# Three slot arrays and bank turns in the order list of a fused attention and MLP kernel

## The chip, the cores and the metric

The kernel runs on one core of a Trainium2 chip. The metric is the device time of one execution in microseconds (us), as the median over several runs. The engines named below are PE (TensorE, matrix products), DVE (VectorE), ACT (ScalarE), POOL (GpSimd) and SP (SyncE, which here only issues DMA transfers). Each engine works through its own instructions in order and waits on semaphores for the others.

## The reference

Sliding-window attention over 8 batches, 8 heads, 576 positions and 64 elements per head. Heads 0 to 3 look back over 32 positions, heads 4 to 7 over every fourth of the last 128. The 4608 rows of 512 that come out go through two dense layers with a leaky ReLU between them.

```python
scores = scale * np.matmul(q, k.transpose(0, 1, 3, 2))
mask_plain = (rel >= 0) & (rel < window)
mask_dil = (rel >= 0) & (rel < window * dilation) & (rel % dilation == 0)
...
scores = np.where(masks[None, :, :, :], scores, -1000000000.0)
attn = np.exp(scores - np.max(scores, axis=-1, keepdims=True))
attn = attn / (np.sum(attn, axis=-1, keepdims=True) + 1e-09)
out = np.matmul(attn, v)
...
x = np.ascontiguousarray(out.transpose(0, 2, 1, 3)).reshape(B * S, H * D)
h = x @ w_in
return (np.maximum(0.01 * h, h) @ w_out).astype(np.float32)
```

Inputs and output are float32. The kernel works in float16 with float32 accumulation.

## The kernel before

**Attention.** A batch is treated in four visits (`VISITS`), each of two heads, one in partitions 0 to 63 and one in 64 to 127; visits 2 and 3 are the dilated heads. For each visit the queries, keys and values lie in one of six *slots*, sections of one array `slots` (lines 321, 433): 576 columns for q, 1152 for k, 1152 for v. Keys and values hold zeros where the other head stands, so that one matrix product serves both heads. `load_qk`, `load_rest` and `load_v` bring float32 data into `stg` and `vst`; `cast` (line 380) turns it into float16 in `nat`, `rest` or the slots.

Batches 0 and 1 (`b < EARLY`) are turned by PE: four 128-column transposes per operand (line 654) into the PSUM bank `tp` (batch 0: keys into `fps[1]`, batch 0's remainder into `hps[1]`), and copies out of that bank into the slot by `move` (line 394, instructions at lines 398 for ACT and 400 for DVE): one for q, two for k, one per head. The remaining 64 positions of a batch go the same way in `turn_rest` (line 689). Batches 2 to 7 are turned by DVE's transpose (lines 619, 624, 631) into `turned`; POOL and others copy from there into the slot. For a dilated visit each head's keys take two copies, one of 512 columns and one of 64.

`unit` (line 722) then makes half a visit: scores by PE (line 775), `exp` by ACT (line 782), for later batches a mask product by DVE (line 786), the sums (lines 793, 810) and the value product (line 793) by PE, `ln` and `exp` of the sums by ACT (lines 818, 820), and the normalised result into `xt` by DVE (line 831).

**MLP.** Rows are taken in twelve chunks of 384. `up` and `up_pair` (lines 841, 872) multiply `w_in` with `xt` into the banks `hps` and others, and ACT writes the leaky ReLU into `gt` (lines 865, 891). `down` (line 904, PE at line 916) multiplies with `w_out` for the first four tiles of 128 rows, in four parts of four matmuls each. The other tiles go in groups of four through a product of seven partial products in place of eight (`group`, PE at line 1006), and the last three chunks' first layer likewise (`up_seven`, PE at line 1275). The latter keeps intermediate blocks in the slots, which are free by then (`scratch`, line 1238). Weights arrive as sixteen loads `w0` to `w15` (`load_w`): `w0` to `w7` are `w_in`, `w8` to `w15` are `w_out`.

**The order.** Nothing is left to a scheduler at run time. All work is recorded as tasks in a `_Plan`: each has one or more engines that could do it with an assumed cost for each, predecessors and a due time. `forward` (line 94) simulates the engines and takes the best task for each in turn; it also picks the engine where there is a choice. `backward` gives new due times from the result, nine passes are made and the shortest is kept. The kernel then issues instructions in that order. Costs are multiplied by factors in `MARGIN`, other ones before and after a planned time `CALM`. `FIRST` (line 29) is a hand-written order of the first loads, where a "." stands for the next piece of values whose loading has begun. `WHEN` gives the due time of each batch's attention.

The waits on semaphores are derived by the framework from the tiles that instructions touch. Two engines that read the same PSUM bank are put one behind the other, in the order of the list. The list before knows nothing of that:

```python
mq = [move(slot(tn, 0, 0, 128, [144, 4], [1, 128]), at(tpb, 0, 128, 0, [128, 4], [1, 128]),
           512, after_q + old, prio, ("DVE", "ACT"), True)]
```

Each such copy may be planned on DVE or ACT, and the copies of one bank as running at the same time on both.

Of the kernel before, what the change touches and what calls it, by code (L numbers as in the profile page):

```python
# [19 lines left out]
WHEN = (0.0, 0.0, 40.0, 70.0, 100.0, 125.0, 150.0, 180.0)  # L20
PASSES = 9
MARGIN = {'ACT': 1.02, 'DVE': 1.062, 'POOL': 1.0, 'PE': 1.0, 'SP': 1.0, 'DMA': 1.133, 'LAND': 1.15}
CALM = 38.8
# [29 lines left out]
class _Task:  # L53
    __slots__ = ("choices", "eng", "lat", "deps", "fn", "prio", "soft", "n", "start", "done",
                 "dur", "left", "ready", "users", "service", "kind", "late", "fixed", "rows", "yields")

    def __init__(self, choices, lat, deps, fn, prio, soft, n, kind):
# [10 lines left out]
        self.yields = []  # L68


class _Plan:
# [22 lines left out]
    def forward(self):  # L94
# [14 lines left out]
        cached = {}  # L109
        while len(order) < len(self.tasks):  # L110
            best = None
            for eng, cand in waiting.items():
# [4 lines left out]
                else:  # L117
# [10 lines left out]
                    for t in cand:  # L128
                        if len(t.choices) > 1:
                            end = max(here, t.ready) + dict(t.choices)[eng] * _margin(eng, here)  # L130
                            if any(max(free.get(e, 0.0), t.ready) + d * _margin(e, here) < end - 0.02
                                   for e, d in t.choices if e != eng):
                                continue
# [131 lines left out]
def kernel(  # L265
# [51 lines left out]
    KB, VB, TS = S, 3 * S, 5 * S  # L317
# [3 lines left out]
    slots = sbuf("slots", [128, NT * TS])  # L321
# [58 lines left out]
    def cast(dst, src, n, deps, prio, engines=("POOL", "DVE"), slow=1.0):  # L380
        cost = {"POOL": 0.15 + n * 0.00102 * slow, "DVE": 0.07 + n * (0.00055 if slow == 1.0 else 0.0011),
# [12 lines left out]
    def move(dst, src, n, deps, prio, eng=("DVE",), dense=False):  # L394
# [8 lines left out]
        return add(tuple((e, cost[e]) for e in eng), None, 0.2, deps, fn, prio)  # L403
# [18 lines left out]
    def clear_slots(which, prio, deps):  # L422
        for i in which:
            t_zero[i] = [clear((("DVE", 0.62), ("POOL", 0.7)),
                               slots[:, i * TS + x:i * TS + x + 2 * S].bitcast(FP32), None, 0.0,
                               prio + 0.01 * i, deps) for x in (KB, VB)]
# [6 lines left out]
    def slot(i, x, p0, p1, *dims):  # L433
        return at(slots, p0, p1, i * TS + x, *dims)
# [8 lines left out]
    def load_qk(b, g, prio):  # L443
# [28 lines left out]
        for j in range(2):  # L472
            nn, n_old = ring("NAT", NNAT, n_users := [])
            na, c_qk = nat[nn], []
            for o in range(2):
                st, s_users = stage[o]
                if early:
# [3 lines left out]
                             ("POOL", "DVE", "ACT") if first else ("POOL", "DVE"))  # L481
# [976 lines left out]
```

## Time and profile before

| | us |
|---|---|
| median of 3 runs | 298.97 |
| lowest and highest run | 298.3, 300.19 |
| the profiled execution | 299.48 |
| its span, first to last instruction | 297.5 |
| PE busy in the span | 284.5 |
| ACT busy, DVE busy | 218.5, 218.1 |
| POOL busy | 144.0 |

The busy times are those of the profiled execution. Busy time of PE includes the passage of a matmul through the array, so that gaps shorter than that do not show. A profile has several views: the page with busy shares in 40 slices of the span, a table by stretches of time, a list of who waited for whom, a timeline of the instructions, and the chain of waits, which goes back from the last instruction to what released each step. "q" behind an engine's name (SPq) is its instruction queue. In a timeline row the first number is the start, the second the duration, both in us from the start of the span; in brackets stands the idle time of the engine just before and what ended it.

### The profile page before, as it was taken

What the parts mean: (1) busy time and instruction counts of PE and PEld (TensorE: products, weight loads), DVE (VectorE), ACT (ScalarE), POOL (GpSimd) and SP (SyncE); (2) the same over time, 40 slices, a digit from 0 to 9 for tenths busy, and PEclk for the clock granted to TensorE, in tenths of its full rate; (3) what the DMA queues carried; (4) which work ended last, traced back from release to release, by engine and by line L of the source; (5) the groups of instructions that cost most, each with busy time, mean ns of one, the idle gap of its engine ahead of it and who ended that gap; (6) DMA issues with size and microseconds to landing.
All of it is one profiled execution on the core that took longest, in us unless ns stands there. A gap on an engine that the chain in (4) does not pass through costs nothing.

```text
span 297.5 us, 7792 instructions
## 1 busy us (share of the span) xinstructions
PE 284.5 (96%) x2975; PEld 225.4 (76%) x2975; DVE 218.1 (73%) x406; ACT 218.5 (73%) x502; POOL 144.0 (48%) x201
## 2 busy tenths in 40 slices
PE   5788989999999999999999999999999999999995
PEld 2665666678667788777777787776789999999984
DVE  6784375975689979738768869999757786587742
ACT  1797469678988884778878876886877787877611
POOL 5545555197778766776885759997100100000000
PEclk9999999999999999999999999999999999999999
DMA  7999999989988989988997998670101210111033
GB/s 216 325 303 402 322 356 249 140 165 169 155 181 175 210 187 149 231 164 173 205 150 197 166 211 160 145 211 3 36 16 53 79 36 2 37 71 39 35 108 106
DMA packets 155973, 47.16 MB, mean 159 GB/s; under 512 B 136736, under 2 KB 153248, under 8 KB 155936
## 3 DMA queue, kind: packets, MB, share of 16 engines
q1 hardware_dynamic: 155248, 46.04, 65.6%
q10 hardware_dynamic: 688, 0.63, 0.7%
q8 instruction: 23, 0.38, 0.6%
q14 instruction: 14, 0.11, 0.1%
HBM read 37.22 MB, written 9.44 MB: 157 GB/s over the span
## 4 chain that ended last, share of the span: by engine, by line
PE 75%; DMA 11%; DVE 5%; SPq 4%; issue 2%; ACT 1%; POOL 1%; DVEq 0%; POOLq 0%
PE hps L850 22%; PE fps L1006 21%; PE tp L1006 8%; PE hps L1275 5%; SPq L373 4%; DMA xt<-in_moe_w_out_dram 3%; PE ops L1275 3%; DMA vst<-in_v_dram 3%; DMA wst<-in_moe_w_in_dram 3%; PE ops L793 3%; PE fps L916 3%; PE hps L879 2%; PE ops L775 2%; DMA stg<-in_k_dram 2%; PE sps L793 1%
## 5 line engine op out<-in xcount | busy, mean ns | idle before, releaser
L850 PE MATMUL hps<-xt,w_in 128*128 128x384 f16 x488 | 95.2, 325 | 1.0 <-DVE w_in L387 0.6
L1006 PEld LDWEIGHTS <-gt 128*128 128x128 f16 x768 | 72.5, 98 | 9.8 <-DVE gt L992 0.4
L865 ACT ACTIVATE gt<-hps 128x384 f16<-128x384 f32 x122 | 59.1, 490 | 20.6 <-PE hps L850 19.5
L850 PEld LDWEIGHTS <-w_in 128*128 128x128 f16 x512 | 45.8, 98 | 23.9 <-issue 1.0
L387 POOL CAST slots<-vst 64x576 f16<-64x576 f32 (+2 forms) x60 | 52.2, 880 | 13.9 <-DVE ee L786 3.9
L387 POOL CAST nat<-stg 128x576 f16<-128x576 f32 (+1 forms) x55 | 41.4, 771 | 20.6 <-PE ops L793 6.8
L1006 PE MATMUL fps<-w_out,gt 128*128 128x256 f16 x368 | 47.0, 272 | 0.0
L786 DVE TENSOR_TENSOR ee<-ee,con 128x384 f16<-128x384 f16 (+1 forms) x48 | 22.2, 464 | 15.5 <-ACT ee L782 15.2
L820 ACT ACTIVATE rc<-rc 128x288 f32<-128x288 f32 x64 | 27.9, 442 | 0.9
L831 DVE TENSOR_TENSOR xt<-ops,rc 128x288 f16<-128x288 f32 x40 | 17.9, 448 | 11.9 <-ACT rc L820 7.7
L775 PEld LDWEIGHTS <-slots 128*128 128x128 f16 x320 | 18.4, 97 | 5.6 <-DVE slots L400 0.9
L400 POOL COPY slots<-turned 64x64 f16<-64x64 f16 (+2 forms) x36 | 19.2, 540 | 6.6 <-DVE turned L619 3.4
L793 PEld LDWEIGHTS <-slots 128*128 128x128 f16 x320 | 17.7, 97 | 4.9 <-issue 1.6
L1035 ACT COPY stg<-fps 128x512 f32<-128x512 f32 (+1 forms) x24 | 12.8, 531 | 11.1 <-PE fps L1006 10.4
L782 ACT ACTIVATE ee<-ops 128x384 f16<-128x384 f32 (+1 forms) x39 | 19.5, 503 | 1.7 <-PE ops L775 0.8
L398 ACT COPY slots<-turned 64x512 f16<-64x512 f16 (+1 forms) x28 | 18.6, 663 | 1.9 <-DVE turned L619 1.5
L818 ACT ACTIVATE rc<-ops 128x288 f32<-128x288 f32 x39 | 15.7, 408 | 5.7 <-PE ops L810 2.8
L802 POOL TENSOR_TENSOR ee<-ee 128x128 f16<-128x128 f16 x9 | 5.4, 601 | 29.2 <-DVE ee L786 29.2
L1302 ACT ACTIVATE gt<-slots 128x384 f16<-128x384 f32 x36 | 18.3, 526 | 0.9 <-DVE slots L1295 0.7
L619 DVE STREAM_TRANSPOSE turned<-nat 128x576 f16<-128x576 f16 x24 | 18.0, 761 | 0.1
L992 DVE TENSOR_TENSOR gt<-gt 128x1024 f16<-128x1024 f16 x21 | 17.1, 819 | 0.4 <-PE fps L1006 0.2
L1275 PEld LDWEIGHTS <-stg 128*128 128x128 f16 x192 | 16.3, 98 | 0.3
(137 smaller groups left out, 554.1 us busy)
## 6 DMA issues: line engine op xcount, KB each, us to landing
out_dram<-osb SPq DMA_DIRECT2D x32, 256.0 KB, 2.7
stg<-in_q_dram SPq DMA_DIRECT2D x48, 144.0 KB, 3.4
stg<-in_k_dram SPq DMA_DIRECT2D x48, 144.0 KB, 3.5
vst<-in_v_dram SPq DMA_DIRECT2D x14, 288.0 KB, 4.2
gt<-in_moe_w_in_dram SPq DMA_DIRECT2D x6, 512.0 KB, 7.1
vst<-in_v_dram SPq DMA_DIRECT2D x24, 128.0 KB, 3.0
stg<-in_q_dram SPq DMA_DIRECT2D x3, 512.0 KB, 9.7
stg<-in_k_dram SPq DMA_DIRECT2D x3, 512.0 KB, 9.5
```

What stands on the lines that cost most here:

```text
L387: return ENG[e].tensor_copy(out=dst, in_=src)
L398: nc.scalar.copy(out=dst, in_=src)
L400: ENG[e].tensor_copy(out=dst, in_=src)
L775: nc.tensor.matmul(p_bank[:, c:c + w], slot(tn, KB + 128 * s, 0, 128, [1, 128]), slot(tn, qx, 0, 128, *qd), start=first or not by_pe, stop ...
L782: lambda e: nc.scalar.activation(out=et[:, 0:n], in_=p_bank[:, 0:n], func=AF.Exp, scale=SCALE), prio)
L786: lambda e: nc.vector.tensor_tensor(out=et[:, 0:n], in0=et[:, 0:n], in1=con[:, table:table + n], op=ALU.mult), prio,
L793: nc.tensor.matmul(at(dst, 0, 128, o, *od), lhs(s), et[:, c:c + w], start=i == 0, stop=i == len(steps) - 1, skip_group_check=True)
L820: lambda e: nc.scalar.activation(out=rt, in_=rt, func=AF.Exp, scale=-1.0), prio)
L850: nc.tensor.matmul(ht[:, 0:n], at(w_in, 0, 128, vi * DFF + j // 2 * 256 + j % 2, [2, 128]), at(xt[m % 2], 0, 128, vi * 1152 + x0 + x, [1, n]),
L865: lambda e: nc.scalar.activation(out=gt[c % NG][:, j * n_c + x:j * n_c + x + n], in_=ht[:, 0:n], func=AF.Prelu, alpha=0.01),
L1006: nc.tensor.matmul(bk[:, x:x + HN], tl[:, off + j * step:off + j * step + 128], rhs(j), start=first and x == 0 and j == 0, stop=j == HJ - ...
L1275: nc.tensor.matmul(b[:, i * HT:i * HT + HT], lhs(v, j0 + i), rhs(v), start=first and i == 0 and v == 0, stop=i == 1 and v == 1, skip_group ...
```

## The change

- `slots` becomes three arrays: `q_in`, `k_in` and `v_of`, of the same total size. The clears at the start stay twelve, the addresses of `scratch` blocks alternate between `k_in` and `v_of`.
- A `move` out of a PSUM bank in `turn` and `turn_rest` carries the name of its bank. `forward` keeps, for each bank, which engine read it last and until when; a task on the other engine is taken as ready only after that.
- The 64-column key copies of the dilated visits of batches 2 to 7 may go to POOL or ACT, before to POOL or DVE.
- The casts of queries and keys for batch 0's dilated visits, and those of the two remainders, get other engines to choose from.
- The list is tuned anew: DVE's assumed cost of a cast goes from 0.00055 to 0.00076 us per element, the due time of batch 3 from 70.0 to 68.5, a factor 1.003 is set on the early loads, and `w12` stands one place earlier in `FIRST`.

As the list is planned anew from these costs, the order of instructions on every engine differs in many places.

```diff
-WHEN = (0.0, 0.0, 40.0, 70.0, 100.0, 125.0, 150.0, 180.0)
+WHEN = (0.0, 0.0, 40.0, 68.5, 100.0, 125.0, 150.0, 180.0)
...
-    return MARGIN[name] if at > CALM else 1.0
-FIRST = ('r0 q01 v01 . q00 w0 v00 . w1 w2 w3 w4 w5 w6 w7 w8 w9 w10 q11 w11 r1 v11 . w12 '
+    return MARGIN[name] if at > CALM else MARGIN['LOAD'] if name == 'DMA' else 1.0
+FIRST = ('r0 q01 v01 . q00 w0 v00 . w1 w2 w3 w4 w5 w6 w7 w8 w9 w10 q11 w11 r1 v11 w12 . '
          'w13 q10 v10 w14 . w15 . . c')
...
+        def when(t, eng):
+            who, done = bank_at.get(t.bank, (eng, 0.0))
+            return t.ready if who == eng or t.bank is None else max(t.ready, done)
...
-                        at = max(here, min(t.ready for t in could))
-                        pick = min(((t.ready + t.soft > at + 1e-9, t.prio, t.n), t)
-                                   for t in could if t.ready <= at + 1e-9)
+                        at = max(here, min(when(t, eng) for t in could))
+                        pick = min(((when(t, eng) + t.soft > at + 1e-9, t.prio, t.n), t)
+                                   for t in could if when(t, eng) <= at + 1e-9)
...
+            if t.bank is not None:
+                bank_at[t.bank] = (eng, t.done)
+                touched.update(("ACT", "DVE"))
...
-    slots = sbuf("slots", [128, NT * TS])
+    q_in = sbuf("q_in", [128, NT * S])
+    k_in = sbuf("k_in", [128, NT * KS])
+    v_of = sbuf("v_of", [128, NT * KS])
...
-        cost = {"POOL": 0.15 + n * 0.00102 * slow, "DVE": 0.07 + n * (0.00055 if slow == 1.0 else 0.0011),
+        cost = {"POOL": 0.15 + n * 0.00102 * slow, "DVE": 0.07 + n * (0.00076 if slow == 1.0 else 0.0011),
...
     def slot(i, x, p0, p1, *dims):
-        return at(slots, p0, p1, i * TS + x, *dims)
+        tl, size, x0 = (q_in, S, 0) if x < KB else (k_in, KS, KB) if x < VB else (v_of, KS, VB)
+        return at(tl, p0, p1, i * size + x - x0, *dims)
...
-                             ("POOL", "DVE", "ACT") if first else ("POOL", "DVE"))
+                             (("DVE", "ACT") if g else ("POOL", "DVE", "ACT")) if first else ("POOL", "DVE"))
...
-                       at(st, 0, 64, o * 512 + 256 * g, [64, 2], [128, 2], [1, D]), 256, [lo] + r_old, prio)
+                       at(st, 0, 64, o * 512 + 256 * g, [64, 2], [128, 2], [1, D]), 256, [lo] + r_old, prio,
+                       ("POOL", "DVE") if b else ("DVE", "ACT"))
...
-                                    at(xk, p0, p1, 512, [1, D]), 64, [tk] + old, prio, ("POOL", "DVE")))
+                                    at(xk, p0, p1, 512, [1, D]), 64, [tk] + old, prio, ("POOL", "ACT")))
...
-                       512, after_q + old, prio, ("DVE", "ACT"), True)]
+                       512, after_q + old, prio, ("DVE", "ACT"), True, key(tpb))]
...
-        tn = (u_tail[1] + i // 3) % NT
+        x = ((-(-u_tail[1] * KS // 768) + i // 2) % 9) * 768
...
-        return slots[:, tn * TS:tn * TS + 2304].bitcast(FP32)[:, i % 3 * 384:i % 3 * 384 + 384], old, users
+        return (k_in, v_of)[i % 2][:, x:x + 768].bitcast(FP32), old, users
```

More of the change, by code (lines that the diff above doesn't have):

```diff
@@ L19 @@
 RAMP = 0.0
-WHEN = (0.0, 0.0, 40.0, 70.0, 100.0, 125.0, 150.0, 180.0)
+WHEN = (0.0, 0.0, 40.0, 68.5, 100.0, 125.0, 150.0, 180.0)
 PASSES = 9
-MARGIN = {'ACT': 1.02, 'DVE': 1.062, 'POOL': 1.0, 'PE': 1.0, 'SP': 1.0, 'DMA': 1.133, 'LAND': 1.15}
+MARGIN = {'LOAD': 1.003, 'ACT': 1.02, 'DVE': 1.062, 'POOL': 1.0, 'PE': 1.0, 'SP': 1.0, 'DMA': 1.133, 'LAND': 1.15}
 CALM = 38.8
@@ L54 @@
     __slots__ = ("choices", "eng", "lat", "deps", "fn", "prio", "soft", "n", "start", "done",
-                 "dur", "left", "ready", "users", "service", "kind", "late", "fixed", "rows", "yields")
+                 "dur", "left", "ready", "users", "service", "kind", "late", "fixed", "rows", "yields", "bank")
     def __init__(self, choices, lat, deps, fn, prio, soft, n, kind):
@@ L68, in __init__ @@
         self.yields = []
+        self.bank = None
 class _Plan:
@@ L402, in move @@
                 "POOL": 0.24 + n * 0.001}
-        return add(tuple((e, cost[e]) for e in eng), None, 0.2, deps, fn, prio)
+        t = add(tuple((e, cost[e]) for e in eng), None, 0.2, deps, fn, prio)
+        t.bank = bank
+        return t
     rings = {}
@@ L519, in load_v @@
             old = [slot_users[b, vi][1] for vi in (2, 3)]
[L520 removed]
+            last = [cast(slot(t0, VB + hh + 1024, 64 * hh, 64 * hh + 64, [KS, 2], [2, D]),
                          at(vs, 0, 64, 1024 + 128 * hh, [D, 2], [1, D]), 128,
@@ L679, in turn @@
                                at(bk, p0, p1, c, [64, 2], [128, 4], [1, D]), 512, after_k + old, prio,
-                               ("DVE", "ACT"), True))
+                               ("DVE", "ACT"), True, key(bk)))
             else:
@@ L683, in turn @@
                                at(bk, p0, p1, c, [16, 8], [1, 16], [128, 4]), 512, after_k + old, prio,
-                               ("DVE", "ACT")))
+                               ("DVE", "ACT"), False, key(bk)))
         q_users += mq
```

32 lines of the change are left out of this document (16 added, 16 removed).

## The prediction, made before the changed kernel ran

> **What bounds the kernel now.** I read the page's slices first, then a table of ten- and twenty-microsecond stretches, then PE's waits, then the chain of waits where PE is idle.
>
> ```profile
> PE 284.5 (96%) x2975; PEld 225.4 (76%) x2975; DVE 218.1 (73%) x406; ACT 218.5 (73%) x502; POOL 144.0 (48%) x201
> PE   5788989999999999999999999999999999999995
> DMA  7999999989988989988997998670101210111033
> ```
> ```profile
> 10.00:20.00 10.00, 7.85 (x128) 6.22 (x126) 8.32 (x20) 9.45 (x22) 5.30 (x10) 1.00 1.01 305
> 20.00:30.00 10.00, 9.01 (x87) 5.78 (x87) 5.27 (x12) 7.64 (x20) 5.32 (x8) 1.00 1.00 385
> 30.00:40.00 10.00, 8.60 (x78) 5.95 (x76) 4.26 (x12) 4.79 (x10) 4.69 (x6) 1.00 1.10 329
> 40.00:50.00 10.00, 9.98 (x129) 7.77 (x128) 6.63 (x16) 8.87 (x23) 6.18 (x10) 1.00 1.11 310
> 50.00:60.00 10.00, 9.91 (x115) 6.23 (x115) 9.02 (x15) 6.95 (x17) 1.98 (x4) 1.00 0.94 155
> 80.00:100.00 20.00, 19.22 (x198) 13.95 (x197) 18.30 (x31) 17.09 (x41) 14.66 (x21) 1.00 0.92 189
> 120.00:200.00 80.00, 80.00 (x804) 60.76 (x802) 62.73 (x106) 64.71 (x148) 60.94 (x80) 1.00 0.90 182
> 200.00:220.00 20.00, 19.62 (x196) 14.83 (x194) 14.92 (x29) 15.35 (x37) 6.89 (x8) 1.00 0.08 29
> 280.00:297.50 17.50, 14.35 (x132) 12.61 (x129) 7.39 (x14) 3.56 (x9) 0.00 (x0) 1.00 0.26 91
> ```
>
> The columns after the stretch and its length are busy time of PE, its weight loads, DVE, ACT and POOL, then the granted clock, the DMA share and GB/s. PE is the bound: over the span it is busy 284.5 of 297.5 us, so 13.0 us are idle in all. These lie in three places. From 10 to 40 us it is 2.15 + 0.99 + 1.40 = 4.54 us, with the DMA engines full (shares 1.01, 1.00, 1.10). From 40 us to the tail it is 0.02 + 0.09 + 0.78 + 0.38 = 1.27 us. The rest is the time before the first data and the tail (17.50 - 14.35 = 3.15 us). The change alters neither the matmuls of the computation nor the last group's order of work, so it can only win idle time of the first two kinds, and the question is which of it is free to go.
>
> **The part at which the change is aimed.** One wait shows the turns at a bank:
>
> ```profile
> 36.70 0.43 DVE L387 CAST w_out<-gt 128x512 f16<-128x512 f32 x1 [1.24 <-DMA gt<-in_moe_w_out_dram]
> 37.04 0.41 DVE L400 COPY slots<-tp 64x512 f16<-64x512 f16 x1
> 37.49 0.58 ACT L398 COPY slots<-tp 128x512 f16<-128x512 f16 x1 [1.82 <-DVE slots L400]
> 37.97 0.88 ACT L891 ACTIVATE gt<-hps 128x384 f16<-128x384 f32 x2
> 38.10 0.43 DVE L400 COPY slots<-tp 64x512 f16<-64x512 f16 x1 [0.65 <-ACT slots L398]
> 38.90 0.33 PE L879 MATMUL hps<-xt,w_in 128*128 128x192 f16 x2 [1.41 <-ACT gt L891]
> ```
>
> DVE's key copy out of `tp` stands behind a weight cast that waits for its DMA. ACT's query copy out of the same bank waits 1.82 us for DVE's turn, with two leaky ReLUs queued behind it; these free the `hps` banks, and PE waits 1.41 us for them. In the list after, the three copies of this visit (batch 1's first) all stand on DVE, ahead of that weight cast; ACT goes from one leaky ReLU to the next. Over both lists, waits of one of the two engines for the other's slot copy out of a bank fall from about 20 to 5. So the wait of 1.41 us goes; that much of the change does what it says.
>
> **What is late next there.** The same stretch has a tie to the loads that no order on the engines moves:
>
> ```profile
> 29.19 2.85 PE L850 MATMUL hps<-xt,w_in 128*128 128x384 f16 x16 [0.41 <-ACT gt L865]
> 31.88 1.03 PE L916 MATMUL fps<-w_out,gt 128*128 128x512 f16 x4
> 32.74 1.46 PE L850 MATMUL hps<-xt,w_in 128*128 128x384 f16 x8
> 34.04 0.39 PE L654 MATMUL tp<-con,nat 128*128 128x128 f16 x4
> 34.22 0.43 DVE L387 CAST nat<-stg 128x512 f16<-128x512 f32 x1 [0.87 <-DMA stg<-in_k_dram]
> 34.26 0.82 PE L879 MATMUL hps<-xt,w_in 128*128 128x192 f16 x8
> 51.16 0.43 DVE L387 CAST w_out<-xt 128x512 f16<-128x512 f32 x1 [0.43 <-DMA xt<-in_moe_w_out_dram]
> 51.17 1.32 PE L916 MATMUL fps<-w_out,gt 128*128 128x512 f16 x4
> ```
> ```profile
> 19.25 8.52 DMA wst<-in_moe_w_in_dram
> 27.79 0.44 DVE w_in L387
> 41.55 9.59 DMA xt<-in_moe_w_out_dram
> 51.19 0.88 POOL w_out L387
> 52.11 0.38 PE fps L916
> ```
>
> The second fence is the chain of waits. It runs through two loads: the last of `w_in`, whose DVE cast begins at 27.79, and the last of `w_out`, landed at 41.55 + 9.59 = 51.14 and cast by POOL until 51.19 + 0.88 = 52.07; PE's last matmul of that `down` part begins at 52.11. SP's order of loads after the change is the same up to that last load but for one exchange (the third `w_out` load into `gt` ahead of a small load of values, 64 KB), and each load waits for one eight places ahead on the queue or for a cast that is done long before. With the DMA engines full from 10 us on, the load lands at 51.1 again.
>
> I then counted PE's list up to that `down` part in both kernels. Apart from filler matmuls (15 before, 13 after) the same work stands ahead of it in both: 64 matmuls of 384 columns and 64 of 192 for the first layer, 28 of `down` with this part included, all 64 transposes of batches 0 and 1, the same scores, sums and value products. So whatever PE wins before, it waits there: at 52.3 us it stands where it stood. The saved 1.41 us turn into other waits, and the list shows where. PE comes to the transposes of batch 1's first keys after 16 and 4 first-layer matmuls and one `down` part: 31.88, plus 0.86 for the `down` part (32.74 - 31.88), plus 0.65 for four matmuls (half of 34.04 - 32.74), is 33.4, plus 0.2 for the query transposes (34.26 - 34.04). The key cast ends at 34.22 + 0.43 = 34.65, so 1.0 us of new wait. By my walk the rest shows ahead of 52 us, up to 1 us in front of the last `w_out` cast.
>
> At that point something may be lost. Before, DVE casts the half that is used first (done 51.59) and POOL the half used second; the matmul of the second half begins at 52.11 and the part ends about 52.3. After, PE needs POOL's half first and DVE's second, so two matmuls follow 52.07 in place of one: one more of 0.22 us (0.86 / 4). I enter this as a loss of 0.2 us. Its bounds are 0, if the load lands a little earlier, and a gain of 1.41 if the load isn't the tie (a rival below).
>
> **The other edits.** Three arrays in place of one change no instruction's size. They take away waits between writers of different sections; the row that such waits would have to show in is PE's, which after 52 us has 1.25 us idle in all, so this edit is in that bound. The exchange of loads brings the small values after 512 KB more of data, 1.4 to 1.7 us later at the 385 to 310 GB/s of these stretches; the first value products of batch 1 stand in PE's list behind ten other tasks there, which hide it, and if they did not, the wait at 52 us would take it up.
>
> ```profile
> L400 POOL COPY slots<-turned 64x64 f16<-64x64 f16 x16 | 4.9, 308 | 2.0 <-DVE turned L619 1.4
> L400 DVE COPY slots<-turned 64x64 f16<-64x64 f16 x8 | 2.6, 324 | 0.2
> L398 ACT COPY slots<-tp 64x128 f16<-64x128 f16 x3 | 0.8, 260 | 0.1
> L398 ACT COPY slots<-turned 64x512 f16<-64x512 f16 x17 | 11.2, 662 | 1.5 <-DVE turned L619 1.2
> ```
>
> The 24 small key copies stand after the change 14 on ACT and 10 on POOL. DVE loses 8 x 0.324 = 2.6 us, POOL 6 x 0.308 = 1.8 us. ACT gains 14. The trace has no such copy on ACT; its nearest row is the 64x128 copy at 260 ns from PSUM, its upper bound the 64x512 one at 662. I take 260: 3.6 us (9.3 at the upper end). All of it lies beside PE work. From 80 to 100 us, where DVE is fullest (18.30 of 20) and PE has 0.78 us idle, ACT has 20 - 17.09 = 2.91 us to spare for some 14/6 = 2.3 such copies per batch. DVE's 2.6 us are relief just there. The recalibrated cast cost moves nothing by itself: it only chooses engines.
>
> [...]
>
> **The sum.** Idle PE time after 52 us that may go: 0.09 + 0.78 + 0.38 = 1.25 us, with these waits behind it:
>
> ```profile
> PE ops L793 <- ACT rc L818: 1.0, 2, 0.6
> PE ops L775 <- DVE xt L831: 0.3, 1, 0.3
> ```
>
> Both are halves of attention in which an ACT or DVE result comes late, between 80 and 100 us and near 206 us. Batch 3, whose visits fall in the first of these, is due 1.5 us earlier in the list after, and DVE is relieved there. All 1.25 us would be the best case; a list planned anew also makes a few waits of its own. I take 0.8 us as gained, with bounds 1.25 gained and nothing. With the 0.2 lost before, the span is 297.5 + 0.2 - 0.8 = 296.9. The profiled execution took 299.48, that is 1.98 more than its span, and lies 0.51 above the median: 296.9 + 1.98 - 0.51 = 298.4 us.
>
> **The rivals.** *The start pays after all.* If the last `w_out` load lands earlier with its neighbours' order changed, the 1.41 us stay won: 298.4 - 1.41 = 297.0. For it: the row of 38.90 is a true wait. Against it: full DMA engines, and equal work ahead of the load. Chance 0.12.
>
> *The gain is given back in the new list.* Waits of about the same size appear elsewhere after 52 us: 299.0 + 0.2 = 299.2. For it: the waits after 52 us were of at most 0.6 us each (the first row above), the kind that any new order moves about. Chance 0.25.
>
> *ACT's queue holds PE up.* The small copies wait on ACT for DVE's transposes, and leaky ReLUs queue behind them, as they did at 37.49; two `hps` banks cover 1.30 us of PE work (34.04 - 32.74). If all 3.6 us come onto the path, it is 299.0 + 3.6 = 302.6. It decides from the point where the copies of a visit exceed ACT's spare time, 2.91 us in the tightest stretch. Against it: 17 copies of 512 columns stand behind the same transposes now and waited 1.5 us in all, and each small copy follows a large one of the same source. Chance 0.13.
>
> **How the numbers follow.** The forecast has chance 0.50 and a range of its own from 297.9 (all 1.25 won) to 298.9 (0.3 won). About 1% is what a measurement here can tell from no change: from 299.0 that is below 296.0 and above 302.0. Only the far end of the first rival reaches below (0.03); most of the third lies above (0.11); the rest is 0.86. The range goes from the first rival with all 1.25 won, 297.0 - 0.45 = 296.5, to the second with half of ACT's copies exposed, 299.2 + 1.8 = 301.0. About 0.15 is left out.
>
> **What would show it.** The last `w_out` load lands within 0.3 us of 51.1, and PE's part behind it ends within 0.5 of 52.3: right on the tie. PE has no wait of over 0.5 us for ACT at 37 to 39 us and a new one near 33.6 for the key cast. Idle PE time from 52 to 280 us falls from 1.25 to about 0.5; if it rises, the second rival holds, and if PE's waits there name ACT's leaky ReLU behind small copies, the third. A landing of `w_out` before 50 us would make the tie wrong.

## The result and the profile after

The changed kernel takes 300.66 us (median of 20 runs, 299.61 to 303.0) where the kernel before, beside it, takes 299.43 (20 runs, 297.08 to 301.39). The ratio is 1.0057 with a 95% interval from 1.0036 to 1.0079: the change costs 1.1 to 2.4 us, and the forecast of 298.4 had the wrong sign. The profiled execution of the changed kernel took 299.93 us, 0.73 below its median, with a span of 298.1. An execution more than 1.5% above the fastest of its kernel stays out of the ratios, and the profiled one of e10 below (304.24 us) was such a one, so that no idle time is given for e10.

The table of stretches of the changed kernel, with the columns of the prediction's (stretch and length; busy time of PE, its weight loads, DVE, ACT, POOL; granted clock, DMA share, GB/s):

```profile
10.00:20.00 10.00, 7.73 (x126) 6.01 (x123) 9.78 (x19) 9.25 (x23) 5.78 (x10) 1.00 1.04 291
20.00:30.00 10.00, 9.19 (x82) 5.67 (x81) 4.84 (x12) 7.12 (x18) 5.82 (x7) 1.00 1.02 400
30.00:40.00 10.00, 9.34 (x84) 6.54 (x83) 5.79 (x18) 5.38 (x12) 5.86 (x9) 1.00 1.08 356
50.00:60.00 10.00, 9.02 (x93) 5.37 (x92) 8.96 (x15) 6.33 (x16) 3.34 (x5) 1.00 0.93 147
80.00:100.00 20.00, 19.48 (x194) 14.27 (x192) 17.39 (x30) 17.65 (x43) 15.82 (x21) 1.00 0.98 199
180.00:200.00 20.00, 19.71 (x197) 14.61 (x195) 19.07 (x28) 18.35 (x42) 13.79 (x18) 1.00 0.71 155
200.00:220.00 20.00, 18.88 (x189) 13.92 (x187) 16.78 (x30) 14.05 (x33) 7.64 (x8) 1.00 0.08 28
280.00:298.10 18.10, 14.97 (x138) 13.18 (x135) 7.98 (x15) 3.97 (x10) 0.00 (x0) 1.00 0.28 95
```

Before 40 us PE is idle for less: 2.27 + 0.81 + 0.66 = 3.74 us from 10 to 40, where it was 4.54. By 52 us nothing of that is left: from 10 to 52 us PE is idle for 4.49 us, where it was 4.56. The tail is unchanged (18.10 - 14.97 = 3.13). Most of the idle time that is new stands between 180 and 220 us: 0.29 + 1.12 = 1.41 us idle, where the kernel before had none up to 200 and 0.38 after. From 80 to 100 us it falls from 0.78 to 0.52, as hoped.

The timeline of the changed kernel (start, duration, engine, line, operation; in brackets the idle time before it and what ended it) has the places on which this document turns:

```profile
33.69 0.40 PE L668 MATMUL tp<-con,nat 128*128 128x128 f16 x4 [0.66 <-DVE nat L397]
49.82 0.87 POOL L397 CAST w_out<-xt 128x512 f16<-128x512 f32 x1 [1.36 <-DMA xt<-in_moe_w_out_dram]
50.74 1.46 PE L931 MATMUL fps<-w_out,gt 128*128 128x512 f16 x6 [0.61 <-POOL w_out L397]
...
188.47 0.24 ACT L408 COPY k_in<-turned 64x64 f16<-64x64 f16 x1
192.99 0.24 ACT L408 COPY k_in<-turned 64x64 f16<-64x64 f16 x1
193.25 0.49 ACT L880 ACTIVATE gt<-hps 128x384 f16<-128x384 f32 x1
193.79 0.81 PE L865 MATMUL hps<-xt,w_in 128*128 128x384 f16 x4 [0.29 <-ACT gt L880]
...
200.74 3.20 POOL L397 CAST v_of<-vst 64x576 f16<-64x576 f32 x3
200.99 1.07 DVE L1007 TENSOR_TENSOR rest<-gt 128x1024 f16<-128x1024 f16 x1
201.98 1.26 DVE L1007 TENSOR_TENSOR pair<-gt 128x1024 f16<-128x1024 f16 x1
203.16 1.26 DVE L1007 TENSOR_TENSOR gt<-gt,gt 128x1024 f16<-128x1024 f16 x1
204.34 0.68 DVE L1007 TENSOR_TENSOR gt<-gt 128x1024 f16<-128x1024 f16 x1
204.95 0.44 DVE L846 TENSOR_TENSOR xt<-ops,rc 128x288 f16<-128x288 f32 x1
205.44 0.35 PE L790 MATMUL ops<-q_in,k_in 128*128 128x64 f16 x5 [0.48 <-DVE xt L846]
```

Four adds of the same form stand on DVE ahead of the product `xt`, which PE waits for. Three of them begin while POOL casts values and take 1.07, 1.26 and 1.26 us; the fourth begins after the last of these three casts (200.74 + 3.20 = 203.94) and takes 0.68. The planner prices each at 0.63 x 1.062 = 0.67 us, so together they take 1.07 + 1.26 + 1.26 + 0.68 - 4 x 0.67 = 1.6 us more than planned. (For the adds of the first four groups of tiles it charges 0.78 in place of 0.63. These four are the first to which the lower price applies.)

### The profile page after: what moved, and what is told of

Read it like the earlier page. It is cut to its first block, busy times and chain, and to the rows that moved or that the text cites. A ratio compares the mean times of both kernels' runs of the same rounds, so it can differ in the third digit from the quotient of the medians.

```text
span 298.1 us, 7773 instructions
## 1 busy us (share of the span) xinstructions
PE 284.7 (95%) x2973; PEld 225.5 (76%) x2973; DVE 220.0 (74%) x403; ACT 219.3 (74%) x511; POOL 140.5 (47%) x195
## 4 chain that ended last, share of the span: by engine, by line
PE 78%; ACT 7%; DVE 6%; DMA 5%; issue 1%; POOL 1%; SPq 0%; ACTq 0%; POOLq 0%
PE fps L1021 22%; PE hps L865 21%; PE tp L1021 8%; DMA stg<-in_k_dram 5%; PE hps L1290 5%; PE hps L894 4%; PE fps L931 3%; PE ops L1290 3%; PE ops L808 3%; ACT gt L880 2%; PE ops L790 2%; ACT k_in L408 1%; PE sps L808 1%; PE sps L1290 1%; PE ops L1021 1%
## 5 line engine op out<-in xcount | busy, mean ns | idle before, releaser
L397 POOL CAST v_of<-vst 64x576 f16<-64x576 f32 (+2 forms) x61 | 54.5, 906 | 17.0 <-DMA vst<-in_v_dram 7.8
L397 POOL CAST nat<-stg 128x576 f16<-128x576 f32 (+1 forms) x54 | 39.7, 749 | 20.1 <-PE ops L808 6.1
L801 DVE TENSOR_TENSOR ee<-ee,con 128x384 f16<-128x384 f16 (+1 forms) x48 | 23.2, 484 | 13.9 <-ACT ee L797 13.5
L408 ACT COPY k_in<-turned 64x512 f16<-64x512 f16 (+2 forms) x44 | 23.1, 529 | 3.0 <-DVE turned L633 2.4
L1050 ACT COPY stg<-fps 128x512 f32<-128x512 f32 (+1 forms) x26 | 13.9, 536 | 12.6 <-PE fps L1021 12.5
L790 PEld LDWEIGHTS <-k_in 128*128 128x128 f16 x320 | 18.8, 97 | 5.6 <-issue 1.0
L817 POOL TENSOR_TENSOR ee<-ee 128x128 f16<-128x128 f16 x12 | 6.3, 532 | 30.1 <-PE hps L1290 16.1
L808 PEld LDWEIGHTS <-v_of 128*128 128x128 f16 x320 | 17.7, 97 | 3.5 <-DVE v_of L397 0.6
L410 POOL COPY k_in<-turned 64x64 f16<-64x64 f16 (+2 forms) x28 | 14.7, 536 | 11.3 <-DVE turned L633 8.4
L1007 DVE TENSOR_TENSOR gt<-gt 128x1024 f16<-128x1024 f16 x21 | 16.2, 776 | 0.9 <-PE fps L1021 0.9
L1021 PE MATMUL fps<-wst,gt 128*128 128x256 f16 x128 | 16.4, 273 | 0.1
```

The costliest lines, as they stand in the source:

```text
L397: return ENG[e].tensor_copy(out=dst, in_=src)
L408: nc.scalar.copy(out=dst, in_=src)
L790: nc.tensor.matmul(p_bank[:, c:c + w], slot(tn, KB + 128 * s, 0, 128, [1, 128]), slot(tn, qx, 0, 128, *qd), start=first or not by_pe, stop ...
L801: lambda e: nc.vector.tensor_tensor(out=et[:, 0:n], in0=et[:, 0:n], in1=con[:, table:table + n], op=ALU.mult), prio,
L808: nc.tensor.matmul(at(dst, 0, 128, o, *od), lhs(s), et[:, c:c + w], start=i == 0, stop=i == len(steps) - 1, skip_group_check=True)
L1021: nc.tensor.matmul(bk[:, x:x + HN], tl[:, off + j * step:off + j * step + 128], rhs(j), start=first and x == 0 and j == 0, stop=j == HJ - ...
```

## The experiments

The planner's list is a sequence of tasks, each with its engine, and both kernels number their tasks alike. So a list can be taken from one kernel and run with the code of the other, or be joined from two; in the diffs such a list is called by its origin. Each experiment but e14 is 6 to 13 executions, with the kernel before beside them on the same chip; e14 is one. PE's idle time in the stretches after 80 us comes out within some hundredths of a microsecond in each profile of one list (200 to 220 us, new list: 1.12, 1.11, 1.12 and 1.14 in the profiles of the changed kernel, e3, e9 and e15), though the runs spread by 3 us; so the place of a loss is read from it, and its size from the ratio.

| kernel | ratio to before, 95% interval | PE idle 80-180 | 180-200 | 200-220 |
|---|---|---|---|---|
| before | | 0.78 | 0 | 0.38 |
| after | 1.0057, 1.0036-1.0079 | 0.52 | 0.29 | 1.12 |
| e1 new code, list before | 1.0022, 0.9996-1.0048 | 0.72 | 0 | 0.38 |
| e2 new list to 52 us | 1.0029, 1.0005-1.0053 | 0.71 | 0 | 0.38 |
| e3 new list from 52 us | 1.0076, 1.0049-1.0104 | 0.53 | 0.31 | 1.11 |
| e4 small copies back | 1.0100, 1.0069-1.0132 | 0.98 | 0 | 1.16 |
| e5 product first | 1.0055, 1.0018-1.0093 | 0.52 | 0.29 | 0.85 |
| e6 casts held back | 1.0008, 0.9973-1.0042 | 0.52 | 0.29 | 0 |
| e7 another constant | 1.0149, 1.0102-1.0196 | 3.05 | 0 | 0.51 |
| e8 no bank turns | 1.0095, 1.0061-1.0129 | 2.77 | 0.05 | 0.59 |
| e9 after again | 1.0075, 1.0046-1.0105 | 0.53 | 0.29 | 1.12 |
| e10 as e6 | 1.0011, 0.9978-1.0045 | - | - | - |
| e11 wider waits, after | 1.0067, 1.0030-1.0104 | 0.78 | 0.29 | 0.80 |
| e12 wider waits, before | 0.9997, 0.9968-1.0027 | 0.71 | 0 | 0.26 |
| e13 e6 and two copies moved | 1.0023, 0.9993-1.0053 | 0.53 | 0 | 0 |
| e15 after on one array | 1.0075, 1.0043-1.0107 | 0.53 | 0.29 | 1.14 |
| e16 as e1 | 0.9987, 0.9957-1.0017 | 0.72 | 0 | 0.38 |
| e17 e13 on one array | 0.9972, 0.9946-0.9998 | 0.53 | 0 | 0 |

### Which part of the list loses

e1, e2 and e3 run the changed code with other lists, e4 puts one edit back:

```diff
 e1
-    order = plan.run()
+    order = list_before
 e2
-    order = plan.run()
+    order = list_after[planned start < 52] + rest_of(list_before)
 e3
-    order = plan.run()
+    order = list_before[planned start < 52] + rest_of(list_after)
 e4
-    order = plan.run()
+    order = list_after, its 24 small key copies on the engines of list_before
```

> The changed code (three arrays, the new scratch places for the last sums) run with the order and the engines of the list before, written into the kernel; one pair of late evictions is moved up because the scratch places differ. Against the kernel before (median 299.4 us), the change cost 0.6%, 1.2 us more than my forecast of a gain of 0.6 and in the other direction. Theory A (the loss is made by the re-planned list after 52 us): no difference, ratio 0.998 to 1.002, and PE's idle time from 52 to 280 us near 1.3 us. Theory B (the three arrays or the scratch places cost it): ratio near 1.004, and the extra idle time after 52 us is here too. Theory C (the small key copies on ACT cost it): no difference, since here they stand on DVE and POOL.

> The changed code with the new list for all work that the plan starts before 52 us, and the order of the list before for all that follows. Theory A: PE's idle time after 52 us is that of the kernel before (near 1.3 us), the start is worth nothing or, as one execution of the changed kernel suggests, up to 0.5 us: 298.9 to 299.4 us where the kernel before takes 299.4, ratio 0.998 to 1.000. Theory B: near 300.6 us. Theory C: as A, because the small key copies all stand after 52 us and are on DVE and POOL here. If the new start itself were the loss: 300.6 us.

> The changed code with the list before for all work planned before 52 us and the new list's order and engines for the rest. Theory A: as slow as the changed kernel or a little slower, 300.6 to 301.1 us, ratio 1.004 to 1.006, with PE idle near 2.3 us from 52 to 280 us, most of it at 180 to 220 us. Theory B and C: 300.6 us too; this run tells A and C from a loss that the start makes (299.4 us).

> The changed kernel with one thing put back: the 24 small key copies run on the engines that had them before (8 on DVE, 16 on POOL, none on ACT); every place in the list stays. Theory A: the other moves of the list after 52 us cost it, so 300.3 to 300.9 us, ratio to the kernel before 1.003 to 1.005; the idle time behind leaky ReLUs near 190 us goes (0.3 us). Theory B: 300.6 us. Theory C: the loss is gone, 299.4 us, ratio 1.000.

The stretches of e1 and then of e3 (columns as above):

```profile
180.00:200.00 20.00, 20.00 (x203) 15.00 (x201) 18.85 (x29) 16.42 (x38) 18.53 (x23) 1.00 0.56 130
200.00:220.00 20.00, 19.62 (x195) 14.75 (x194) 15.09 (x30) 15.35 (x38) 7.35 (x8) 1.00 0.08 29
```
```profile
180.00:200.00 20.00, 19.69 (x194) 14.58 (x193) 19.08 (x30) 17.68 (x41) 13.05 (x18) 1.00 0.60 137
200.00:220.00 20.00, 18.89 (x187) 13.86 (x186) 17.16 (x30) 14.56 (x34) 8.39 (x9) 1.00 0.08 29
```

The new idle time goes with the part of the new list after 52 us: e3 has it all, e1 and e2 have none of it. The ratios say the same less sharply. That of e3 is as high as the changed kernel's, and e1 cannot be told from the kernel before; but e2 lies 0.05 to 0.53% above it, where no loss was expected, and its idle time after 80 us (1.09 us against 1.16) does not hold that. e3 and e4 too are slower than theory A had said (1.0076 and 1.0100 against at most 1.006 and 1.005), and slower than their idle time after 80 us accounts for. Theory C (all of it from the small copies) falls with e4, which is no faster than the changed kernel. It did take the 0.29 us at 180 to 200 away, as expected, but from 80 to 180 us 0.52 became 0.98, of which 0.35 us are a new wait for one of these copies on POOL (at 90.65).

### What is late at 200 us

```diff
 e5, VectorE's order
   L1007 pair <- gt
+  L846  xt <- ops, rc
   L1007 gt <- gt, gt
   L1007 gt <- gt
-  L846  xt <- ops, rc
 e6, GpSimd's order
-  L397 v_of <- vst  x5
+  L397 v_of <- vst  (waits for VectorE's fourth add)
+  L397 v_of <- vst
   L817 ee <- ee
   L410 k_in <- turned
+  L397 v_of <- vst  x3
```

> The changed kernel with one move in VectorE's order near 202 us: the product that makes xt (L846), which PE waits for at 205.4, stands ahead of the last two of the four 128x1024 adds (L1007) and not behind them. Theory A1 (the loss at 200 to 220 us is made by those adds ahead of the product): PE's wait of 0.48 us goes, PE's idle time at 200 to 220 falls from 1.11-1.16 (three kernels with the new list there) to 0.4-0.7, and the time falls by as much, ratio to the kernel before 1.003 to 1.005 in place of 1.0057. Rival (another engine is late there too, the product only the last to be seen): idle time stays within 0.2 of 1.1 us.

> The changed kernel with VectorE's order as it is, but GpSimd's value casts of 200.7 to 203.9 us held back behind the fourth add (one of them waits for it, three more go behind GpSimd's next two other operations). Theory A2 (the adds are late because GpSimd works beside them: 0.68 us with GpSimd idle, 1.07 to 1.26 with it): the four adds take 2.7 to 2.9 us in place of 4.3, the product begins 1.3 to 1.5 us earlier, PE's wait of 0.48 us goes and idle time at 200 to 220 falls to 0.4-0.7. Rival (the adds are slow for another reason): they keep 1.1 to 1.3 us each, idle time stays near 1.1.

The timeline of e6 in the same place:

```profile
200.85 0.67 DVE L1007 TENSOR_TENSOR rest<-gt 128x1024 f16<-128x1024 f16 x1
201.45 0.68 DVE L1007 TENSOR_TENSOR pair<-gt 128x1024 f16<-128x1024 f16 x1
202.05 0.68 DVE L1007 TENSOR_TENSOR gt<-gt,gt 128x1024 f16<-128x1024 f16 x1
202.65 0.68 DVE L1007 TENSOR_TENSOR gt<-gt 128x1024 f16<-128x1024 f16 x1
203.25 0.44 DVE L846 TENSOR_TENSOR xt<-ops,rc 128x288 f16<-128x288 f32 x1
203.45 1.73 POOL L397 CAST v_of<-vst 64x576 f16<-64x576 f32 x2 [2.92 <-issue]
204.65 0.35 PE L790 MATMUL ops<-q_in,k_in 128*128 128x64 f16 x5
205.59 0.21 DVE L817 TENSOR_TENSOR ee<-ee 128x128 f16<-128x128 f16 x1
```

The last row has its counterpart in the changed kernel, where a fourth cast (205.74 to 206.97) runs beside it:

```profile
206.20 0.79 DVE L817 TENSOR_TENSOR ee<-ee 128x128 f16<-128x128 f16 x1
```

All four adds take 0.67 to 0.68 us, the product begins 1.70 us earlier (0.14 of that because the first add does), PE does not wait, and the whole of the 1.12 us from 200 to 220 is gone, more than expected: I had left 0.4 to 0.7 us there. Part of the surplus is a second loss of the same kind: the sum of two blocks of `ee` (L817), which PE waited for by 0.24 us at 207.04, takes 0.21 us in place of 0.79. The ratio comes back to 1.0008. e5 met neither theory: PE's wait of 0.48 us went, but 0.85 us stay. The first two adds keep their 1.07 and 1.25 us, and PE now waits for DVE's mask product (L801, 0.21 us) and, as before, for the sum (L817, 0.24 us). So the order alone is not the cause; the time that DVE loses beside POOL is.

Then e6 once more beside the changed kernel, and two tries to make a rule of it:

```diff
 e11 (after) and e12 (before), share()
-            if t.eng == "DVE" and t.kind in ("m",):
+            if t.eng == "DVE" and t.kind in ("m", "A", "T"):
```

> The changed kernel itself, beside the other three runs on one chip: ratio to the kernel before 1.004 to 1.008 as in its own 20 runs (1.0057), PE idle 1.3 to 1.5 us at 180 to 220 us.

> The changed kernel with the GpSimd casts held back behind the fourth add, once more. Theory A2: the loss of the changed kernel is mostly this place, so the ratio to the kernel before is 0.998 to 1.002, and 1.1 us (0.4%) below the changed kernel of this call; PE idle at 200 to 220 us at most 0.2. Rival (its first time was a good draw of the loads): as the changed kernel, within 0.3 us.

> The changed kernel with its own rule by which a GpSimd cast waits for VectorE's mask product (24 waits) widened to VectorE's large adds and input sums too (41 waits), everywhere after 55 us, the order kept. Theory A2 (GpSimd beside the adds makes the losses): the adds that take 0.9 to 1.27 us with GpSimd become fewer (20 of 64 have GpSimd beside all of it), PE idle at 200 to 220 below 0.8, time 0.3 to 1.0 us below the changed kernel's. Rival (held back GpSimd work is late for others): new waits for VectorE's transposes and for value casts, as slow as the changed kernel or up to 1 us slower.

> The same widening (43 waits) in the kernel before, whose idle time after 52 us is 0.09 + 0.78 + 0.38. Theory A2: the wait at 206 us (0.38) goes, at most 0.5 us faster than the kernel before, ratio 0.998 to 1.000. Rival: GpSimd's held back work costs as much as it gives, ratio 1.000 to 1.003.

Side by side on one chip the changed kernel has 1.0075 (from 1.0046) and the kernel with the casts held back 1.0011 (to 1.0045): the intervals just fail to meet. That settles the place for most of the loss. The rule is another matter. In e11 idle time from 200 to 220 falls only to 0.80, at the edge of what was expected, and between 80 and 220 us PE waits for such a sum on POOL (L817) twice, 0.9 us in all, where it was once 0.3; its ratio cannot be told from the changed kernel's. e12 cannot be told from the kernel before. Holding POOL back helps at a place where its work is not due, and a rule by kind of instruction does not know that.

e14 asks the question of the two engines apart. It adds work that nothing uses, late in the program, where POOL is otherwise idle:

```diff
 GpSimd's order, six times, after the VectorE operation two or three ahead of an add
+  nc.gpsimd.tensor_copy(out=at(vst[1].bitcast(FP16), 0, 64, 0, [128, 9], [2, D]),
+                        in_=at(vst[0], 0, 64, 0, [D, 9], [1, D]))   x2
```

> The changed kernel with twelve GpSimd casts added that nothing uses, of the size of a value cast, two at a time near six of VectorE's 128x1024 adds between 248 and 287 us, where GpSimd is idle and all 20 adds took 0.68 to 0.69 us. Theory A2: an add that falls beside such a cast takes 1.0 to 1.3 us, the others 0.68; the span grows by 0.5 us or more only if PE waits for these adds. Rival (the slow adds at 200 us were slow for their operands or ScalarE beside them): all stay at 0.68 to 0.70 us.

From its timeline:

```profile
262.91 0.69 DVE L1007 TENSOR_TENSOR rest<-gt 128x1024 f16<-128x1024 f16 x1 [0.98 <-ACT gt L1317]
263.74 0.83 POOL L1417 CAST vst<-vst 64x576 f16<-64x576 f32 x1 [9.71 <-DVE rest L1007]
264.12 0.93 DVE L1007 TENSOR_TENSOR pair<-gt 128x1024 f16<-128x1024 f16 x1
264.62 1.12 POOL L1417 CAST vst<-vst 64x576 f16<-64x576 f32 x1
264.98 1.26 DVE L1007 TENSOR_TENSOR gt<-gt,gt 128x1024 f16<-128x1024 f16 x1
268.16 0.68 DVE L1007 TENSOR_TENSOR gt<-rest,gt 128x1024 f16<-128x1024 f16 x1
...
280.95 0.69 DVE L1007 TENSOR_TENSOR gt<-gt 128x1024 f16<-128x1024 f16 x1
281.04 1.28 POOL L1417 CAST vst<-vst 64x576 f16<-64x576 f32 x1 [7.80 <-DVE pair L1007]
281.56 1.26 DVE L1007 TENSOR_TENSOR rest<-gt 128x1024 f16<-128x1024 f16 x1
282.39 1.12 POOL L1417 CAST vst<-vst 64x576 f16<-64x576 f32 x1
282.74 1.26 DVE L1007 TENSOR_TENSOR gt<-pair,gt 128x1024 f16<-128x1024 f16 x1
283.92 0.68 DVE L1007 TENSOR_TENSOR gt<-gt,gt 128x1024 f16<-128x1024 f16 x1
```

Of the 20 adds late in the program, the ten that begin while an added cast runs take 0.79 to 1.26 us, and the other ten keep 0.68 to 0.69. The run took 300.41 us (one run), its span is 0.5 us longer. The operands are of the same kind in both. POOL beside the adds is by itself the cause, and which of the two began first decides who loses. The add of 264.12 began while the cast of 263.74 ran, which ended at 264.56; the add ended at 265.05, 0.49 us later. The add of 280.95 began ahead of the cast of 281.04 and took its 0.69 us; the cast took 1.28 us, where the one of 263.74 took 0.83.

### Whether the list was bad luck, and the bank turns

```diff
 e7
-MARGIN = {'LOAD': 1.003, ...
+MARGIN = {'LOAD': 1.0, ...
 e8, move()
-        t.bank = bank
+        t.bank = None
```

> The changed kernel with one constant of the planner changed that no theory of the hardware speaks of: the early loads' cost factor 1.003 becomes 1.0, and the list is planned anew. Theory A (the loss is that of one list among many): another list (113 of 1946 tasks change their engine), two adds ahead of the product near 203 in place of four, idle time at 200 to 220 below 0.8 us, and a time anywhere from 298.4 to 301 us. Rival (a lasting cost of the change's parts: key copies on ACT, three arrays, bank turns): 300.3 to 301.0 us with idle time of about 2.3 us after 52 us once more.

> The changed kernel planned without the turns at PSUM banks, everything else of the change kept. My prediction's tie to the loads: the bank turns are worth nothing by themselves, so the time lies with that of the run of the other constant, within 0.6 us, and the last load of w_out lands at 50.5 to 51.5 us all the same. Rival (the turns win the 1.41 us that were seen at 38.9): slower by 1 us or more than the run of the other constant, with PE idle from 10 to 52 us up by about as much. Theory A: idle time after 52 us is another list's again, anywhere from 1 to 2.5 us.

The stretches of e7:

```profile
80.00:100.00 20.00, 17.99 (x185) 13.40 (x183) 16.65 (x28) 16.88 (x41) 13.56 (x18) 1.00 0.96 197
100.00:120.00 20.00, 19.65 (x215) 16.49 (x212) 16.48 (x28) 13.63 (x32) 15.65 (x23) 1.00 0.93 184
120.00:180.00 60.00, 59.31 (x592) 44.56 (x591) 42.24 (x71) 48.98 (x115) 41.31 (x59) 1.00 0.86 167
200.00:220.00 20.00, 19.49 (x193) 14.47 (x192) 17.13 (x31) 15.95 (x37) 9.03 (x10) 1.00 0.12 42
```

A constant changed by 0.3%, on early loads alone, gives a list that takes 1.5% more than the kernel before, and its idle time lies elsewhere: 2.01 us at 80 to 100, 0.51 at 200 to 220 (the latter as theory A had said). My band for it (298.4 to 301) was too narrow: it took 303.52. No lasting cost of the change's parts has this pattern. What a re-planned list gains or loses after 52 us is of the size of this study's whole effect and larger. e8, planned without the bank turns, is not slower than e7: its ratio is 1.0095 against 1.0149, with intervals that overlap. PE idle from 10 to 52 us is 3.16 us in it against 2.75. The rival (1.41 us won by the turns) falls; that the turns are worth a few tenths cannot be excluded from two lists that differ everywhere. Two of my own expectations for e8 failed as well: the time is not within 0.6 us of e7's, and the casts of the last `w_out` load begin at 49.8 us, not after 50.5.

### The rest of the loss, and the three arrays

```diff
 e13
-    order = plan.run()
+    order = list of e6, the small key copies of 188.5 and 193.0 us on GpSimd
 e15 (list of the changed kernel), e17 (list of e13)
-    q_in = sbuf("q_in", [128, NT * S])
-    k_in = sbuf("k_in", [128, NT * KS])
-    v_of = sbuf("v_of", [128, NT * KS])
+    slots = sbuf("slots", [128, NT * TS])
...
```

e16 is e1 once more.

> The changed kernel with the GpSimd casts held back behind the fourth add, and with the two small key copies that ScalarE runs at 188.5 and 193.0 us on GpSimd in place of it. Theory (what is left of the loss at 180 to 200 us, PE's wait of 0.29 for a leaky ReLU, comes from these small copies on ScalarE, rival 3 of the prediction in small): PE idle at 180 to 200 falls from 0.29 to 0, and at 200 to 220 it stays at 0; the ratio to the kernel before is 0.997 to 1.002, by idle time after 80 us alone 0.5 us below the kernel with the casts held back. Other theory (the large key copies or the copies out of the banks hold ScalarE): 0.29 stays.

> The changed kernel's list, engines and constants with the one array `slots` and the scratch places of the kernel before: only the edit of three arrays is undone. Theory B' (beside the loss at 180 to 220 us the three arrays cost 0.5 to 0.9 us ahead of 80 us, as the ratios of the kernels with them suggest once their idle time after 80 us is taken off): ratio to the kernel before 1.003 to 1.005 in place of 1.0057 and 1.0075 for the changed kernel. Theory A alone: 1.005 to 1.007, and PE idle 1.4 us at 180 to 220 us as in the changed kernel.

> The run of the changed code with the list before once more (first time 1.0022, interval 0.9996 to 1.0048). Theory B': 1.002 to 1.004 again, so that the two together exclude 1. Theory A alone: 0.999 to 1.001.

> The new list on the one array of before, with the GpSimd casts held back behind the fourth add and the two small key copies on GpSimd: by idle time after 80 us (0.53 against 1.16 in the kernel before) 0.4 us below the kernel before if the start is worth nothing, ratio 0.997 to 1.001. Theory B': 0.998 to 1.000, so below the same kernel with three arrays (1.0023). Theory A alone: 1.000 to 1.002, as that one.

The stretches of e13:

```profile
180.00:200.00 20.00, 20.00 (x197) 14.97 (x196) 19.25 (x29) 17.00 (x39) 14.57 (x21) 1.00 0.59 137
200.00:220.00 20.00, 20.00 (x206) 15.22 (x204) 16.95 (x32) 15.26 (x37) 6.46 (x9) 1.00 0.08 29
```

Two copies of 0.24 us off ACT, and the wait of 0.29 us for the leaky ReLU is gone. Theory B' falls: on one array the new list has 1.0075, what the changed kernel had beside e10, and e16 gave 0.9987 where it should have given 1.002 to 1.004 (with e1, 1.0005 in the mean). So the three arrays cost nothing that these runs can tell. e13 and e17 have the same list, with 0.53 us idle from 80 to 220 us where the kernel before has 1.16. e17 took 297.82 us, ratio 0.9972, just below 1 by its interval and below what either theory had said; e13 gave 1.0023. This one pair, run on two chips, would put 0.5% on the arrays; the other two comparisons (the changed kernel with e15, and e1 with e16 against the kernel before) put nothing on them, and I follow these. The two together are then level with the kernel before, and some 0.6% below the changed one. A version that beats both is not shown.

## Why the prediction was wrong

**PE as the bound.** Right. PE is busy for 284.7 of the changed kernel's 298.1 us, and the losses that could be placed are idle time of PE.

**The bank wait goes.** Right in its place: nothing in the changed kernel's timeline at 37 to 39 us waits for the other engine's copy out of the bank.

**The tie to the loads, and 0.2 us lost.** Right: PE waits 0.61 us for POOL's half of the last `w_out` cast (row of 50.74), the 0.8 us that it wins before 40 us are gone by 52 us, and e2, which has the new start alone, is no faster than the kernel before. The new wait for the key cast is there at 33.69, 0.66 us against 1.0. But the sign by which I wanted to check it was badly chosen. The load was to land within 0.3 us of 51.1, and a landing before 50 was to make the tie wrong; DVE's and POOL's casts of it began at 49.8, and PE waited all the same. In e1 and e16, which are one kernel, the casts of this load began at 51.86 and 49.56. The 0.2 us are too small for any of these runs; e2's interval would allow a loss of 0.1 to 1.6 us at the start.

**The other edits hidden.** Right for the arrays. For the small copies the price was right (14 on ACT at 241 ns, 3.4 us in all, against 260 and 3.6), but not all of them lay beside PE work: 0.29 us came through a leaky ReLU at 193.79. That is the third rival, on a tenth of its scale. The mean of 324 ns for such a copy on DVE was misread. Of the eight, four take 0.13 to 0.18 us; the other four take 0.25 to 0.75 us, and each of these began while POOL ran a cast or a copy and ended 0.04 us after it (the copy of 137.44, for one, took 0.53 us). At 0.13 to 0.18 us the eight would take 1.0 to 1.4 us in place of the 2.6 that I counted as relief for DVE (an estimate from those four). The row shows, ahead of the change, the collision that the next paragraphs are about.

**The gain of 0.8 us after 52 us, bounds 1.25 and nothing.** This is the step that failed. Idle time from 52 to 280 us did not fall from 1.25 to about 0.5: it rose to 0.42 + 0.52 + 0.29 + 1.12 = 2.35 (52 to 80, 80 to 180, 180 to 200 and 200 to 220 us). In place of a gain the runs showed 0.29 us behind two small copies on ACT (e13) and 1.12 - 0.38 = 0.74 us more behind work of DVE that POOL's casts hold up (e6, e14). The part that I counted on most, 80 to 100 us, did improve, by 0.26. The sum fails because its lower bound was "nothing". I had written that a new list makes a few waits of its own, and gave them no price. The second rival took the gain back and stopped there (299.2); it had the right cause, a new order, and too small a size: the forecast gain of 0.8 us turned into a loss of 1.1 to 2.4, of which rows of idle time after 52 us hold 2.35 - 1.25 = 1.1. That the measured 300.66 us lies inside the range stated, below 301.0, is luck. That end of the range came from half of ACT's copies exposed, and these cost 0.29 us.

The price could have been read in the trace of before. Here is its timeline at the wait near 206 us, which the sum counted as idle time to be won:

```profile
201.37 0.68 DVE L992 TENSOR_TENSOR rest<-gt 128x1024 f16<-128x1024 f16 x1
201.85 2.96 POOL L387 CAST slots<-vst 64x576 f16<-64x576 f32 x3 [0.58 <-POOL slots L387]
203.05 1.07 DVE L992 TENSOR_TENSOR gt<-gt,gt 128x1024 f16<-128x1024 f16 x1
204.04 1.26 DVE L992 TENSOR_TENSOR pair<-gt 128x1024 f16<-128x1024 f16 x1
205.23 0.68 DVE L992 TENSOR_TENSOR gt<-rest,gt 128x1024 f16<-128x1024 f16 x1
206.12 0.45 DVE L831 TENSOR_TENSOR xt<-ops,rc 128x288 f16<-128x288 f32 x1
206.61 0.34 PE L775 MATMUL ops<-slots 128*128 128x64 f16 x5 [0.26 <-DVE xt L831]
```

One form of add takes 0.68, 1.07, 1.26 and 0.68 us within 5 us, slow where it begins while POOL casts. The wait for `xt` was such a delay already, with two slow adds ahead. The new list put a third slow add there, and 0.38 us of idle time became 1.12. I asked which idle time could go, with durations as fixed numbers; I did not ask which durations depend on what stands beside them, which a new list shuffles. The kernel itself pointed at it: `share`, the function that e11 and e12 edit, is there in both kernels to hold POOL's casts back behind DVE's mask products and the sums that follow them.

Add by add the traces show it more sharply than the groups of a profile do. Over all profiles but e10's, 179 adds begin with more than 0.2 us of a 64x576 value cast still to run; 174 of them end 0.48 to 0.50 us after that cast (19 of 20 in the two profiles of the kernel before and the changed kernel). An add alone takes 0.68 us, so all of it but about 0.2 us comes after the cast. The other way round, a value cast that begins during an add ends 0.68 to 0.71 us after it, and alone takes 0.82 to 0.84. These adds have both inputs in SBUF. The product `xt`, with one input in PSUM, shows no such delay: of the changed kernel's 64, 27 begin while POOL casts and take 0.41 to 0.46 us, and the 21 that meet nothing on POOL take 0.43 to 0.46.

How much is explained: from 180 to 220 us the idle rows hold 1.41 - 0.38 = 1.03 us more than before. Over all stretches after 80 us it is 1.93 - 1.16 = 0.77 us, as 80 to 180 us improved. The ratios of the new list (1.0057, 1.0075 and, on one array, 1.0075) say 1.7 to 2.2 us. So about 1 us of the loss (an estimate, with 0.5 us to either side by the intervals) stands in no idle row after 80 us, and its cause stays open. e2 would put some of it on the new start; e3, which has the old start, is no faster. Taking away the slow adds and the two copies brings the ratio from 1.0057 and 1.0075 to between 0.9972 and 1.0023, that is 1.0 to 3.1 us, where the idle rows lose 1.41.

## What to carry to other kernels

When a change makes a planner order everything anew, forecast the new order as a draw of its own: price what it may lose, not only what it may win, and size that from re-plans with a harmless constant changed (the one made here moved the time by 1.5%). A duration that varies within one group of the profile is a warning; find what stands beside the slow ones before using the mean, and look at repeated instructions one by one. If a new list is a little slower, compare the idle time of the bounding engine by stretch, which repeats to a few hundredths of a microsecond where the total spreads by three, and repair the place by hand.

## What the runs showed of the hardware

An add of two 128x1024 fp16 operands in SBUF takes 0.68 us on VectorE with GpSimd idle (31 of the 64 in the changed kernel: 0.678 to 0.693) and up to 1.27 there with GpSimd casting. If a 64x576 cast has more than 0.2 us still to run when the add begins, the add ends 0.48 to 0.50 us after the cast (174 of 179). The cast is held up in the same way when it begins second: 0.83 us alone, 1.11 to 1.28 in e14.

The last weight load, in nearly the same order of loads and with the DMA engines full (shares of 1.00 to 1.11 from 10 to 50 us in the profile of before), let its casts begin anywhere from 49.4 to 53.2 us in sixteen profiles. e1 and e16 are the same kernel, with spans of 298.0 and 296.1 us and the same 1.10 us of idle time from 80 to 220 us, so the difference between these two arose ahead of 80 us. The loads need not be all of it: in e1's profile the granted clock from 10 to 20 us was 0.84, in e16's it was 1.00 from 10 to 52 us.
